# Moving the FFT pieces of an interleaved FFT + MLP kernel: pair distance in one batch, inverse-pair lag and first-stage start in the others

## The chip, the core and the metric

The kernel runs on one NeuronCore of a Trainium2 chip. The metric is the device time of one execution in microseconds (us), lower is better. The core has a matrix engine (TensorE, PE in the profile; its weight loads are listed as PEld), a vector engine (VectorE, DVE), a scalar engine (ScalarE, ACT), GpSimd (POOL) and a queue for transfers (SyncE, SP). Each of them works through its own instructions in order. PSUM is the memory that PE writes; here it is cut into eight banks of 128 x 512 float32.

## The reference

The input is x (8 batches, 3008 positions, 256 channels). A real FFT runs along the positions, the spectrum is multiplied by a filter, and the inverse FFT follows. The result, 24064 rows of 256, goes through a two-layer MLP with PReLU.

```python
def _attn_ref(x, filt_r, filt_i):
    X = np.fft.rfft(x, axis=1)
    F = (filt_r + 1j * filt_i)[None, :, :]
    Y = X * F
    y = np.fft.irfft(Y, n=x.shape[1], axis=1)
    return y.astype(np.float32)

def _moe_ref(x, w_in, w_out, alpha):          # w_in 256 x 2048, w_out 2048 x 256
    h = x @ w_in
    g = np.maximum(h, 0.0) + alpha * np.minimum(h, 0.0)
    return (g @ w_out).astype(np.float32)
```

## The kernel before

**The FFT of a batch** is factored as 3008 = 47 x 64 and done with matmuls in float16. `Fft` has these pieces, each one bank of PSUM from the pool `psF`, which has two banks:

- first stage, `piece_a`, 16 of a batch (letter a): one matmul of 512 columns from `xs` (L164), evicted by ACT into `asb` (L238);
- forward pair, `piece_b`, 12 of a batch (b): two matmuls of 256 columns (L184), then on DVE `ww` (L188) and `uu` (L189), both reading the bank, and two DMAs on POOL that swap the halves of `ww` into `sw` (L191);
- swap-add, `piece_s`: `uu += sw` on DVE (L196), in batches 2 to 7;
- inverse pair, `piece_c`, 12 of a batch (c): two matmuls of 256 columns on `uu` (L209), evicted by ACT into `v` (L238). Batch 1 has no swap-add and uses four matmuls, on `uu` and on `sw`;
- last stage, `piece_d`, 16 of a batch (d): four matmuls of 94 columns (L231), evicted by ACT into `yT` (L238).

Between first stage and forward pairs the data go through DRAM to be transposed: `save_a` writes `asb`, `turn_a` reads it back into `at`. Between inverse pairs and last stage `turn_c` does the same for `v` and `zt`, in four quarters. All of these are DMAs on the SP queue, which also issues the stores of the result. Loads of `xs` and the `sw` swaps are issued on POOL.

**The MLP** runs over 48 blocks of tokens, 12 for each pair of batches (11 of 512 tokens and one of 384), 16 steps to a block, 768 steps in all. In step j, `up(j)` computes one 128-row slice of the hidden layer (two matmuls, L414), into one half of a double bank `hps`; after odd j, ACT copies both halves to `gtb` (L420) and DVE applies the PReLU (two instructions `m`, L423, and an add, L424). `down(j)` does a sixteenth of the second layer of the block before (four matmuls of 256 columns, L433; three after a block of 384). At the middle and the end of a block of 512 its result is evicted by ACT into `osb` (L438) and stored.

**The order of the work** is written out by hand. `plan` maps a step to a list of pieces that are issued ahead of `up` in this step. So a piece of an odd step is evicted ahead of this step's `gtb` copy on ACT, and one of an even step behind the `gtb` copy of the step before; a step that is a multiple of 8 also has the `osb` eviction of the step before in front of it, save in narrow blocks.

`plan_fft(b, a0, ga, ta, b0, gap, add, lag, d0, quarters, x_at)` places batch b: first-stage piece i at `a0 + ga*i`; `turn_a` at `ta`; forward pair kp at `b0 + gap*kp` (rounded to even distances where `add` is set); the swap-add `add` steps and the inverse pair `lag` steps later; `turn_c` of a quarter one step after its third inverse pair; last-stage piece i from `d0` on; `x_at` are the steps in which the next batch's `xs` are loaded. For batches 3 to 7 everything is placed against p = 96(b-1): pairs at p+5, 9, 15, 19, 25, 29, 35, 39, 45, 49, 55 and 59. While these run, the first stage of batch b+1 runs from p+26 on. Batch 0 is handled ahead of the loop and in its first 47 steps.

Of the kernel before, what the change touches and what calls it, by code (L numbers as in the profile page):

```python
# [64 lines left out]
def kernel(  # L65
# [59 lines left out]
    def load_x(b, c):  # L125
        xs = p_x.tile([2 * N1, 8 * D], FP16, name="xs")
        for h in range(2):
            nc.gpsimd.dma_start(out=xs[h * N1 : h * N1 + N1], in_=xrow(b, h, c))  # L128
        return xs
# [314 lines left out]
    def put(step, fn, *args):  # L444
        plan.setdefault(step, []).append((fn, args))

    def plan_fft(b, a0, ga, ta, b0, gap, add, lag, d0, quarters, x_at):
        f = Fft(b)
        for i in range(16):
            put(int(a0 + ga * i), f.piece_a, i, on_act)  # L450
        for c in range(4):
            put(int(a0 + ga * (4 * c + 3)), f.save_a, c)
            if b + 1 < NB:
                put(x_at[c],
                    lambda b=b, c=c: xc.update({(b + 1, c): load_x(b + 1, c)}))
        for q in range(quarters):
            w = NK1 // quarters
            put(ta, f.turn_a, nc.sync, w * q, w * q + w)
        bs = [b0 + (2 * int(gap * kp / 2) if add else int(gap * kp)) for kp in range(12)]
        for kp in range(12):  # L460
            put(bs[kp], f.piece_b, kp)
            if add:
                put(bs[kp] + add, f.piece_s, kp)
            put(bs[kp] + lag, f.piece_c, kp, on_act)
        for q in range(4):
            put(bs[3 * q + 2] + lag + 1, f.turn_c, q)
        for i in range(16):
            put(d0 + min(i, 4) + 2 * max(i - 4, 0), f.piece_d, i, on_act)
# [9 lines left out]
    for i in range(4):  # L478
        put(17 + 3 * i, neg, 6 * i, 6 * i + 6)
    put(29, lambda: nc.gpsimd.dma_start(out=filt_s[64:128], in_=filt_s[0:64]))  # L480
    plan_fft(1, 16, 1, 32, 44, 2.5, 0, 6, 92, 4, (20, 24, 73, 74))
    plan_fft(2, 66, 2, 97, 109, 4.5, 8, 13, 187, 4, (110, 114, 118, 122))
    for b in range(3, NB):
        p = 96 * (b - 1)
        plan_fft(b, p - 70, 2.5, p - 27, p + 5, 5, 8, 13, p + 91, 1, (p + 6, p + 10, p + 16, p + 20))

    prev = None
    step = 0
# [43 lines left out]
```

## Time and profile before

| | |
|---|---|
| median of 3 runs | 799.88 us (799.49 to 799.96) |
| the profiled execution | 799.77 us |
| its span in the profile | 798.0 us |
| granted PE clock, mean | 0.996 |
| start and batch 0, 0 to 38.5 us: PE busy | 31.5 of 38.5 us |
| batch 1's pairs, steps 0 to 79, 38.5 to 126.5 us: PE busy | 83.8 of 88.0 us |
| batch 2's pairs, 126.5 to 220.5 us: PE busy | 92.3 of 94.0 us |
| batches 3 to 6, 220.5 to 602 us: PE busy | 380.1 of 381.5 us |
| batch 7 and the tail, 602 to 798 us: PE busy | 190.4 of 196.0 us |

The shares are those of PE matmuls. A matmul's end is modelled, and matmuls overlap, so short waits show smaller than they are: the distance between the starts of two neighbouring matmuls tells the wait. A line of the page's groups has: line, engine, operation, output and inputs, shapes, count; after the first bar the busy time in us and the mean of one in ns; after the second bar the engine's idle time ahead of these instructions, and what ended most of it. A line of the list of waits has: who waited, for whom, us in total, times, longest. A line of the timeline has: start and length in us, engine, line, operation, tiles, count, and in brackets the idle time before it and its releaser. SP's lines there are instructions that issue transfers; their length is that of issuing, not of the transfer.

### The profile page before, as it was taken

The numbers are of one execution on the slowest core, as the hardware profiler recorded it, in microseconds if no ns is written. First come the engines' busy times: TensorE is split into PE (matmuls) and PEld (weight loads), VectorE is DVE, ScalarE is ACT, GpSimd is POOL, SyncE is SP. The second block draws the span as 40 slices with busy tenths as digits, with TensorE's granted clock in tenths as the row PEclk, the third lists the DMA queues.
The fourth block names the chain that finished last, engine by engine and source line by source line (L and its number), as shares of the span: only waits on it lengthen the run. The fifth ranks groups of instructions, "written<-read, shape, count | busy, mean of one in ns | idle before, by whom it ended". The sixth has DMA issues, their size and how long they took to land.

```text
span 798.0 us, 16169 instructions
## 1 busy us (share of the span) xinstructions
PE 778.0 (97%) x5980; PEld 542.0 (68%) x5980; DVE 646.1 (81%) x1449; ACT 597.9 (75%) x836; POOL 140.6 (18%) x269
## 2 busy tenths in 40 slices
PE   6999999999999999999999999999999999999997
PEld 6756667666667666766667666766667766776665
DVE  4897986799879887798877988799877999777773
ACT  3788668877777887788878877788877867686663
POOL 7510240132103210032102321032100221000000
PEclk9999999999999999999999999999999999999999
DMA  9967358674655447475483545654484243511111
GB/s 191 202 141 193 96 131 209 168 159 129 157 141 116 115 121 177 126 139 132 117 208 81 123 127 139 180 110 114 122 180 116 54 106 85 137 39 28 41 40 53
DMA packets 94247, 100.59 MB, mean 126 GB/s; under 512 B 11320, under 2 KB 81992, under 8 KB 94040
## 3 DMA queue, kind: packets, MB, share of 16 engines
q1 hardware_dynamic: 79512, 68.80, 32.6%
q0 software_dynamic: 14656, 30.75, 19.8%
q8 instruction: 47, 0.77, 0.4%
q14 instruction: 32, 0.26, 0.1%
HBM read 56.26 MB, written 46.66 MB: 129 GB/s over the span
## 4 chain that ended last, share of the span: by engine, by line
PE 87%; ACT 4%; DVE 3%; DMA 3%; issue 2%; SPq 1%; POOL 1%; ACTq 0%; DVEq 0%; POOLq 0%
PE op L433 38%; PE hps L414 37%; PE psF L164 3%; PE psF L231 3%; PE psF L184 2%; PE psF L209 2%; ACT gtb L420 2%; DMA xs<-in_x_dram 1%; DMA a_dram<-asb 1%; DVE ww L188 1%; ACT osb L438 1%; DVE m L423 1%; PE hps L281 1%; DVE uu L189 1%; ACT asb L238 1%
## 5 line engine op out<-in xcount | busy, mean ns | idle before, releaser
L420 ACT ACTIVATE gtb<-hps 128x1024 f16<-128x1024 f32 (+1 forms) x384 | 385.5, 1005 | 127.4 <-PE hps L414 127.0
L433 PE MATMUL op<-wout_s,gtb 128*128 128x256 f16 x3008 | 451.1, 272 | 0.6 <-DVE gtb L424 0.6
L414 PE MATMUL hps<-yT,win_s 128*128 128x512 f16 (+1 forms) x1536 | 449.1, 374 | 0.4 <-ACT gtb L420 0.2
L433 PEld LDWEIGHTS <-gtb 128*128 128x128 f16 x3008 | 293.3, 98 | 189.6 <-DVE gtb L424 0.9
L423 DVE TENSOR_SCALAR m<-gtb,alm_s 128x512 f16<-128x512 f16 (+1 forms) x768 | 237.6, 351 | 100.0 <-ACT gtb L420 98.0
L424 DVE TENSOR_TENSOR gtb<-gtb,m 128x1024 f16<-128x1024 f16 (+1 forms) x384 | 261.6, 681 | 24.8 <-PE hps L414 0.9
L191 POOL DMA_DIRECT2D sw<-ww x168 | 88.0, 529 | 494.4 <-DVE ww L188 485.4
L414 PEld LDWEIGHTS <-win_s 128*128 128x128 f16 x1536 | 145.0, 98 | 31.9 <-issue 4.0
L238 ACT ACTIVATE asb<-psF 96x512 f16<-96x512 f32 x112 | 66.4, 593 | 17.5 <-PE psF L164 17.4
L238 ACT ACTIVATE yT<-psF 128x376 f16<-128x376 f32 x120 | 58.1, 484 | 22.8 <-PE psF L231 22.3
L438 ACT ACTIVATE osb<-op 128x512 f32<-128x512 f32 x96 | 56.1, 584 | 6.1 <-issue 3.2
L188 DVE TENSOR_TENSOR ww<-psF,filts_s 128x512 f16<-128x512 f32 x84 | 57.5, 684 | 0.4 <-PE psF L184 0.3
L189 DVE TENSOR_TENSOR uu<-psF,filt_s 128x512 f16<-128x512 f32 x84 | 57.2, 681 | 0.0
L238 ACT ACTIVATE v<-psF 128x512 f16<-128x512 f32 x84 | 49.9, 594 | 3.3 <-PE psF L209 3.3
L164 PE MATMUL psF<-xs,wf_s 94*96 94x512 f16 x112 | 42.7, 381 | 3.0 <-DVE uu L189 1.3
L231 PE MATMUL psF<-wi_s,zt 96*128 96x94 f16 x504 | 41.9, 204 | 0.9 <-ACT yT L238 0.7
L128 POOL DMA_DIRECT2D xs<-in_x_dram x64 | 34.6, 549 | 26.8 <-PE psF L164 15.0
L231 PEld LDWEIGHTS <-zt 96*128 96x128 f16 x512 | 35.5, 97 | 5.1 <-issue 1.5
L184 PE MATMUL psF<-at,twf_s 128*128 128x256 f16 x168 | 32.0, 272 | 3.0 <-ACT v L238 2.1
L209 PE MATMUL psF<-uu,twi_s 128*128 128x256 f16 x168 | 33.4, 273 | 0.0
L196 DVE TENSOR_TENSOR uu<-uu,sw 128x512 f16<-128x512 f16 x72 | 30.1, 418 | 0.0
L209 PEld LDWEIGHTS <-twi_s 128*128 128x128 f16 x192 | 18.6, 98 | 2.5 <-DVE uu L189 0.4
(57 smaller groups left out, 195.0 us busy)
## 6 DMA issues: line engine op xcount, KB each, us to landing
out_dram<-osb SPq DMA_DIRECT2D x128, 128.0 KB
xs<-in_x_dram POOLq DMA_DIRECT2D x64, 188.0 KB, 4.5
a_dram<-asb SPq DMA_DIRECT2D x28, 384.0 KB
sw<-ww POOLq DMA_DIRECT2D x168, 64.0 KB, 2.1
v_dram<-v SPq DMA_DIRECT2D x112, 96.0 KB
zt<-v_dram SPq DMA_DIRECT2D x28, 384.0 KB
at<-a_dram SPq DMA_DIRECT2D x20, 384.0 KB
at<-a_dram SPq DMA_DIRECT2D x32, 96.0 KB
```

Source lines behind the costliest of these rows:

```text
L164: nc.tensor.matmul(ps[0:96], wf1_s, xs[:, o : o + 512], start=True, stop=True)
L188: nc.vector.tensor_mul(ww, px, filts_s[:, 2 * kp : 2 * kp + 2])
L189: nc.vector.tensor_mul(uu, px, filt_s[:, 2 * kp : 2 * kp + 2])
L191: nc.gpsimd.dma_start(out=sw[o : o + 64], in_=ww[64 - o : 128 - o])
L209: nc.tensor.matmul(pv[:, kh], twi_s[:, k1], u[:, kh], start=u is us[0], stop=u is us[-1])
L231: nc.tensor.matmul(ps[:, m], self.zt[:, 8 * g + 4 * mh + m, dh * 128 : dh * 128 + 128], wi3_s, start=True, stop=True)
L238: nc.scalar.activation(o, i, AF.Copy)
L414: nc.tensor.matmul(self.hps[:, j % 2, 0:tn], win_s[:, kt, j * 128 : (j + 1) * 128], yT[:, kt, self.t0 : self.t0 + tn], start=(kt == 0), st ...
L420: nc.scalar.activation(g[:, :, 0:tn], self.hps[:, :, 0:tn], AF.Copy)
L423: nc.vector.tensor_scalar(m[:, i, 0:tn], g[:, i, 0:tn], 0.0, a, OP.min, OP.mult)
L424: nc.vector.tensor_add(g[:, :, 0:tn], g[:, :, 0:tn], m[:, :, 0:tn])
L433: nc.tensor.matmul(self.op[:, si % 2], self.gts[k][:, 128 * si : 128 * si + 128], wout_s[:, k], start=(k == 0), stop=(k == 15))
```

## The change

Three calls of `plan_fft` get other numbers. No instruction is added or removed on any engine.

```diff
-    plan_fft(1, 16, 1, 32, 44, 2.5, 0, 6, 92, 4, (20, 24, 73, 74))
-    plan_fft(2, 66, 2, 97, 109, 4.5, 8, 13, 187, 4, (110, 114, 118, 122))
+    plan_fft(1, 16, 1, 32, 40, 3, 0, 6, 92, 4, (20, 24, 74, 75))
+    plan_fft(2, 66, 2, 97, 109, 4.5, 8, 12, 187, 4, (110, 114, 118, 122))
     for b in range(3, NB):
         p = 96 * (b - 1)
-        plan_fft(b, p - 70, 2.5, p - 27, p + 5, 5, 8, 13, p + 91, 1, (p + 6, p + 10, p + 16, p + 20))
+        plan_fft(b, p - 68, 2.4, p - 27, p + 5, 5, 8, 12, p + 91, 1, (p + 6, p + 10, p + 16, p + 20))
```

- Batch 1 (the second batch): forward pairs at steps 40, 43, 46, ..., 73 instead of 44, 46, 49, 51, ..., 71; inverse pairs still 6 steps later, so 46 to 79 instead of 50 to 77; `turn_c` at 53, 62, 71, 80 instead of 56, 63, 71, 78. Two loads of `xs` are issued one step later.
- Batches 2 to 7: inverse pairs and `turn_c` one step earlier. The inverse pairs of batches 3 to 7 go from p+18, 22, 28, 32, ... (even steps) to p+17, 21, 27, 31, 37, 41, 47, 51, 57, 61, 67, 71 (odd steps).
- Batches 3 to 7: first-stage pieces, counted by the batch whose pairs run beside them, at p+28, 30, 32, 35, 37, 40, 42, 44, 47, 49, 52, 54, 56, 59, 61, 64 instead of p+26, 28, 31, 33, 36, 38, 41, 43, 46, 48, 51, 53, 56, 58, 61, 63.

## The prediction

> **What bounds the kernel now.** I read the page's busy shares, then who waited for whom on TensorE (PE), then the timeline around those waits, then SyncE's queue.
>
> ```profile
> PE 778.0 (97%) x5980; PEld 542.0 (68%) x5980; DVE 646.1 (81%) x1449; ACT 597.9 (75%) x836; POOL 140.6 (18%) x269
> L423 DVE TENSOR_SCALAR m<-gtb,alm_s 128x512 f16<-128x512 f16 (+1 forms) x768 | 237.6, 351 | 100.0 <-ACT gtb L420 98.0
> L189 DVE TENSOR_TENSOR uu<-psF,filt_s 128x512 f16<-128x512 f32 x84 | 57.2, 681 | 0.0
> ```
>
> PE is the bound; the change leaves its instructions as they are and only reorders them, so time can come only from waits that go or come. A psF bank is freed after a forward pair by `uu`, last of two VectorE (DVE) instructions of 0.68 us, queued behind `m` and the add of the MLP.
>
> ```profile
> PE psF L184 <- ACT v L238: 2.1, 6, 0.3
> PE psF L164 <- DVE uu L189: 1.3, 2, 0.7
> PE psF L184 <- DVE uu L189: 1.0, 1, 1.0
> PE psF L164 <- DMA xs<-in_x_dram: 0.9, 1, 0.9
> ```
>
> Each is a wait for one of the two psF banks (the last too: its instruction names the bank, its releaser ended at 166.17 us, and PE moved at 166.22). These rows count idle time after a modelled matmul end; from start to start a wait costs about 0.16 us more. I use start to start below.
>
> ```profile
> 377.58 1.02 ACT L420 ACTIVATE gtb<-hps 128x1024 f16<-128x1024 f32 x1 [0.45 <-PE hps L414]
> 378.50 0.59 ACT L438 ACTIVATE osb<-op 128x512 f32<-128x512 f32 x1
> 378.98 0.60 ACT L238 ACTIVATE v<-psF 128x512 f16<-128x512 f32 x1
> 379.64 0.38 PE L184 MATMUL psF<-at,twf_s 128*128 128x256 f16 x2 [0.35 <-ACT v L238]
> ```
>
> This is step p+49 of batch 4 (p = 96(b-1) = 288). An inverse pair and a first-stage piece both stood at p+48, right after `gtb` and `osb`; ScalarE (ACT) reached `v` only after both, and the next forward pair waited from 379.12 to 379.64: 0.52 us. It recurs at 189 to 191 us and once in each of batches 3 to 6.
>
> **A step's length on PE.** Up starts at 345.86, down at 346.29, the next piece would be due at 346.73: 0.87 us a step. A first-stage piece, a forward pair and an inverse pair add 0.22 each, a last-stage piece 0.17 (345.69 to 345.86), an inverse pair of batch 1 (four matmuls) 0.43.
>
> **Batches 3 to 7: waits that come.** Forward pairs stay at p+5, 9, 15, 19, ..., 59. Inverse pairs come one step earlier, at p+17, 21, 27, 31, 37, ... In the changed program's order the bank of a pair is asked for again two steps later, not three, at eight places in a batch. The place is visible in the trace already:
>
> ```profile
> 345.45 0.68 DVE L188 TENSOR_TENSOR ww<-psF,filts_s 128x512 f16<-128x512 f32 x1
> 346.05 0.68 DVE L189 TENSOR_TENSOR uu<-psF,filt_s 128x512 f16<-128x512 f32 x1
> 345.86 0.60 PE L414 MATMUL hps<-yT,win_s 128*128 128x512 f16 x2
> 346.79 0.39 PE L209 MATMUL psF<-uu,twi_s 128*128 128x256 f16 x2
> ```
>
> The inverse pair that now starts at 346.79 (p+18) is due at 345.86 in the new order (p+17). Its bank is free at 346.05 + 0.68 = 346.73, plus 0.05 for the semaphore as at 346.79. So it waits 0.9 us, and everything behind it on PE with it. In the old order one more step stood between, so the wait was 0.06.
>
> I did the same for all eight: end of `uu` after the pair's first matmul, read pair by pair from the timeline, plus 0.03 to 0.05, minus PE's way to the next user of the bank. p+17 after the pair at p+15: 2.33 - 2.12, so 0.24 (in batches 4 and 6, whose previous block is the narrow one: 2.89 against 2.01, the 0.9 above). p+21: 2.10 - 2.12, nothing as it stands; but the inverse pair that lay between the up and the pair at p+19 now lies ahead of that up, so PE reaches the pair 0.22 earlier in DVE's cycle: 0.27. p+31: 2.22 - 2.17, and the same shift: 0.27. p+37 (the first-stage piece there): 2.74 - 2.39, less what ACT gains as the piece at p+33 goes: 0.19. p+41: 2.45 - 2.17 and the shift: 0.46. p+47 and p+57: 2.54 - 2.17, but first-stage pieces newly between give PE 0.22 back, and less ACT work ahead of `gtb` some more: 0.10 each. p+61: 2.25 - 2.39, with 0.43 of pieces moved ahead of the up: 0.30. Sum 1.93 us; from the trace unshifted it would be 1.8. In batches 4 and 6 it is 1.93 + 0.66 = 2.59; I keep 0.27 at p+21 there, since the 0.9 us wait just before lets DVE catch up. Batch 7 has no first stage beside it: 0.5. Together 2 x 1.93 + 2 x 2.59 + 0.5 = 9.5.
> Gone: the 0.52 at p+49 in batches 3 to 6, because inverse pairs now stand on odd steps and are evicted ahead of `gtb`: -2.1. Net **+7.4**.
>
> **Batch 2 and the start of batch 3's first stage (+2 steps).** Gone: 1.11 at step 122 (piece and inverse pair in one step, 165.11 to 166.22), 0.52 at 145 and 0.51 at 153 (same pattern as above), 0.28 and 0.07 at 159 and 149: -2.5. New behind `uu`, by the same reckoning: 0.16 at 129 (2.27 after its pair against 2.17), 0.19 at 133 (2.33 against 2.39, with the shift), 0.36 at 151 (2.32 against 2.17, with the shift). At 157 an inverse pair, a forward pair and a piece in one step, where the piece waits for its own step's `v`: that ends 0.11 + 0.27 + 0.04 + 0.59 after the inverse pair starts, PE is there after 0.43: 0.58. Net **-1.2**.
>
> **Batch 1.** Gone: 1.13 at step 46 (a pair two steps after the pair at 44), and 0.80, 0.86, 0.28 at 66, 70, 72: -3.1. With a distance of 3 each bank has three steps. New, by the same rows: 0.24 at 43 (`uu` 3.20 after a pair on an even step, PE's way 2.99); 0.58 at 46, where a last-stage piece, an inverse and a forward pair meet and the forward pair waits for `yT` behind `gtb` (2.05 after the up of step 45 starts, due at 1.47); 0.64 at 70, where a piece waits for its own step's `v` behind `gtb` (2.16 after that up, due at 1.52); 0.28 at 73, behind `gtb`, `osb` and `asb` (2.64, due at 2.36). Net **-1.3**. The first pair's data: SyncE issues the four quarters of `at` from 74.1 to 81.7 us, the first quarter's four from 74.1 to 75.9; the pair moves from 82.3 to 78.5. With 2.1 us to landing (the `sw` row) it is in time by 0.5, with 4.5 (`xs`) late by 1.9. I take 0, as a 96 KB piece is nearest to `sw`'s 64 KB.
>
> **Batch 1's last quarter.** Its writes move from step 78 to 80 in SyncE's queue, past the three stores of the block that ends at step 79; the zt reads queue behind them, and the first last-stage piece (step 92, at 136.76) behind those.
>
> ```profile
> 124.30 1.92 SPq L218 DMA_DIRECT2D v_dram<-v  x4
> 130.16 1.72 SPq L224 DMA_DIRECT2D zt<-v_dram  x4
> 406.42 2.00 SPq L218 DMA_DIRECT2D v_dram<-v  x4
> 410.00 1.73 SPq L224 DMA_DIRECT2D zt<-v_dram  x4
> ```
>
> Stores behind a block's end finish issuing 4.4 us after the start of its last step (104.53 to 108.92), so the writes start at 125.43 + 4.4 = 129.8 instead of 124.3. The reads follow 3.6 to 5.9 later and take 2.1 to 4.5 to land: 135.5 to 140.2 against 136.76, a wait of 0 to 3.4. With the middles, 4.7 and 3.3: **+1.0**.
>
> **Sum.** 7.4 - 1.2 - 1.3 + 1.0 = +5.9 on the profiled run's 799.77 us (span 798.0 and 1.8 around it; 0.1 below the median of 799.88): **805.7 us**. Some 45 new waits, each good to about 0.06 in the same direction, make +-2.5; the zt wait -1.0/+2.4.
>
> The Trainium skill ("TensorE: Matmul & The Clock Gate", section on psum-queue depth-cycling) tells of a kernel whose many short idles between matmul groups let the clock gate swing. The trace here speaks against it: from 80 to 120 us, with four waits of 0.3 to 1.1 us, the granted clock is 1.00.
>
> **Rivals.**
> - *DVE is early enough* (faster). The place is the bank behind `uu`, two steps after a forward pair; it decides at 2.1 us from pair to end of `uu`. If DVE stays under it, the 9.5 and 0.7 (steps 129, 133, 151) and 0.24 fall away: 805.7 - 10.4 = 795.3. For it: two places read 2.10 and 2.22. Against: 2.33 to 2.89 elsewhere. 0.06.
> - *Waits pay for each other*: a wait lets DVE catch up, so that the next one is spared, and half of the 9.5 remains: 801.0. For it: batch 4's 2.89 falls to 2.49 by p+25. Against: ten steps there last 10.4 us and hold 9.3 of DVE work (five times `m` and add at 1.25, two pairs at 1.20, two swap-adds at 0.33), so there is little room. 0.13.
> - *The early transfers are late*: zt at its upper end and the first `at` quarter 1.9 late: 805.7 + 2.4 + 1.9 = 810.0. For it: DMA share is 0.98 to 1.07 at 132 to 139 us. Against: the middles. 0.12.
> - *The clock drops* in the 56-step stretches of batches 3 to 7 to the 0.83 shown at 10 to 20 us: five times 60 us at 0.83 last 61 us longer, 867. 0.01.
> - *The change does less than it says*: the new `a` positions change nothing if banks, not steps, set the order; then only batch 1 and 2 count, 799.77 - 2.5 + 1.0 = 798.3. 0.02.
>
> **Numbers.** Forecast 0.66, from 802.5 to 808.5. Range 802.0 to 809.6: it takes in the size errors and most of the late-transfer case. No change can be told within 0.2%, 798.3 to 801.5. Faster 0.07; same 0.07, about half of the second rival; slower 0.86.
>
> **What would show it.** Waits of PE at L209 and L164 for `uu`, some 0.1 to 0.9 us, at p+17, 21, 31, 37, 41, 61 in each batch, and none of L184 for `v` at p+49; batch 4's and 6's p+17 the longest. Steps 16 to 64 of a batch some 1.4 us longer (2.1 in 4 and 6), the rest of the batch the same; steps 64 to 80 shorter; PE idle at step 92 for zt. It is wrong if those waits for `uu` are missing, or if blocks without FFT pairs change length.

## The result, and the profile after

The changed kernel takes 808.03 us (median of 4 runs, 807.34 to 809.6), the kernel before 799.68 (4 runs): a ratio of 1.0108, interval 1.0091 to 1.0126. It is slower by 8.4 us; the forecast was 805.7, in a range of 802.0 to 809.6. The profiled execution is the quickest of the four, 807.34 us, with a span of 805.5; its first `up` starts 0.9 us earlier than in the profile of before (37.6 against 38.5). The change moves nothing ahead of step 40, and the loads came at the same time: TensorE starts on the last `xs` of batch 0 at 12.79 us, against 12.75. What differs is the granted clock, in the stretch from 10 to 20 us 1.00 here and 0.83 there. So the differences below are taken from the first `up` on.

The same lines of the page, of the changed kernel, and the line of the inverse pair (L209):

```profile
PE 781.5 (97%) x5980; PEld 538.6 (67%) x5980; DVE 647.0 (80%) x1449; ACT 599.1 (74%) x836; POOL 140.4 (17%) x269
L423 DVE TENSOR_SCALAR m<-gtb,alm_s 128x512 f16<-128x512 f16 (+1 forms) x768 | 237.7, 351 | 108.1 <-ACT gtb L420 107.3
L189 DVE TENSOR_TENSOR uu<-psF,filt_s 128x512 f16<-128x512 f32 x84 | 57.2, 682 | 0.0
L209 PE MATMUL psF<-uu,twi_s 128*128 128x256 f16 x168 | 33.7, 274 | 4.9 <-DVE uu L189 4.5
```

The line of the inverse pair in the kernel before:

```profile
L209 PE MATMUL psF<-uu,twi_s 128*128 128x256 f16 x168 | 33.4, 273 | 0.0
```

Counts and durations have not moved; the busy shares tell nothing. What is new is idle time ahead of the inverse pair, which had none before. The list of PE's waits, of the changed kernel:

```profile
PE psF L209 <- DVE uu L189: 4.5, 15, 0.8
PE psF L231 <- DMA zt<-v_dram: 1.6, 1, 1.6
PE psF L164 <- ACT v L238: 1.0, 2, 0.5
PE psF L209 <- DMA sw<-ww: 0.8, 1, 0.8
```

The waits of the forward pairs (L184) for `v` and `uu` are gone, and the inverse pair's waits for `uu` of an earlier pair have come, with one for zt and one for `sw`. The row shows 15 waits, but from start to start there are more: 0.16 us of each wait hide under a matmul's modelled end, and the row holds no idle time under 0.15 us. From start to start, 37 waits from step 120 on end 0.05 to 0.06 us behind the end of a `uu`.

The place that the prediction used, batch 4's p+17 (TensorE's and VectorE's timeline, changed kernel):

```profile
346.18 0.69 DVE L188 TENSOR_TENSOR ww<-psF,filts_s 128x512 f16<-128x512 f32 x1
346.78 0.68 DVE L189 TENSOR_TENSOR uu<-psF,filt_s 128x512 f16<-128x512 f32 x1
...
346.42 0.33 PE L231 MATMUL psF<-wi_s,zt 96*128 96x94 f16 x4
347.52 0.39 PE L209 MATMUL psF<-uu,twi_s 128*128 128x256 f16 x2 [0.77 <-DVE uu L189]
```

`uu` ends at 347.46, the inverse pair starts 0.06 later. The four last-stage matmuls ahead of it take 0.17, so it was due at 346.59: a wait of 0.93 us, forecast 0.9. And p+49 of the same batch, on ScalarE and TensorE:

```profile
380.10 0.60 ACT L238 ACTIVATE v<-psF 128x512 f16<-128x512 f32 x1 [0.50 <-PE psF L209]
380.59 0.58 ACT L238 ACTIVATE asb<-psF 96x512 f16<-96x512 f32 x1
381.07 1.02 ACT L420 ACTIVATE gtb<-hps 128x1024 f16<-128x1024 f32 x1
...
382.04 0.38 PE L184 MATMUL psF<-at,twf_s 128*128 128x256 f16 x2
```

`v` and `asb` are now evicted ahead of `gtb`, two steps before the forward pair, which has no wait left in its line. SyncE's queue around batch 1's last quarter:

```profile
125.74 2.33 SPq L396 DMA_DIRECT2D out_dram<-osb  x3
128.12 2.35 SPq L218 DMA_DIRECT2D v_dram<-v  x4
132.19 2.63 SPq L224 DMA_DIRECT2D zt<-v_dram  x4
```

The three stores stand ahead of the writes. The last stage, due at 134.84, started at 136.64.

Where the time went, as the difference (changed minus before) of the distance between the starts of `up` at both ends of a stretch:

| steps | forecast | measured |
|---|---|---|
| 32 to 80, batch 1's pairs | -1.3 | -1.0 |
| 80 to 96, wait for zt | +1.0 | +1.8 |
| 96 to 176, batch 2's pairs | -1.2 | -0.8 |
| 208 to 256 and 400 to 448, batches 3 and 5 | +1.4 each | +1.6 each |
| 304 to 352 and 496 to 544, batches 4 and 6 | +2.07 each | +2.3 each |
| 592 to 608, batch 7 | +0.5 | +0.5 |
| all other stretches | 0 | 0.0 |
| sum (the rows are rounded) | +5.9 | +8.4 |

### The profile page after: what moved, and what is told of

The parts are those of the page before. It is cut to its first block, busy times and chain, and to the rows that moved or that the text cites. A ratio compares the mean times of both kernels' runs of the same rounds, so it can differ in the third digit from the quotient of the medians.

```text
span 805.5 us, 16163 instructions
## 1 busy us (share of the span) xinstructions
PE 781.5 (97%) x5980; PEld 538.6 (67%) x5980; DVE 647.0 (80%) x1449; ACT 599.1 (74%) x836; POOL 140.4 (17%) x269
## 4 chain that ended last, share of the span: by engine, by line
PE 74%; DVE 12%; ACT 7%; issue 3%; DMA 3%; SPq 1%; POOL 0%; ACTq 0%; DVEq 0%; POOLq 0%
PE op L433 32%; PE hps L414 31%; ACT gtb L420 4%; DVE m L423 4%; DVE gtb L424 3%; PE psF L209 3%; PE psF L164 2%; DVE ww L188 2%; DVE uu L189 2%; PE psF L231 2%; PE psF L184 1%; ACT asb L238 1%; DMA xs<-in_x_dram 1%; DMA v_dram<-v 1%; ACT osb L438 1%
## 5 line engine op out<-in xcount | busy, mean ns | idle before, releaser
L209 PE MATMUL psF<-uu,twi_s 128*128 128x256 f16 x168 | 33.7, 274 | 4.9 <-DVE uu L189 4.5
L184 PE MATMUL psF<-at,twf_s 128*128 128x256 f16 x168 | 32.1, 272 | 0.2
L209 PEld LDWEIGHTS <-twi_s 128*128 128x128 f16 x192 | 16.7, 98 | 12.8 <-DVE uu L189 10.2
```

The lines of the kernel that those rows point to most:

```text
L209: nc.tensor.matmul(pv[:, kh], twi_s[:, k1], u[:, kh], start=u is us[0], stop=u is us[-1])
```

## The experiments

Three theories stood against each other. One: the loss is the psF bank, asked for two steps after a forward pair while `uu` still reads it. Two: it is the inverse pair's own data, the swap-add being a step too late. Three: it is the new places of batch 1's pairs and of the first stage.

**e1: the lag alone undone.**

```diff
-    plan_fft(2, 66, 2, 97, 109, 4.5, 8, 12, 187, ...)
+    plan_fft(2, 66, 2, 97, 109, 4.5, 8, 13, 187, ...)
-        plan_fft(b, p - 68, 2.4, p - 27, p + 5, 5, 8, 12, p + 91, ...)
+        plan_fft(b, p - 68, 2.4, p - 27, p + 5, 5, 8, 13, p + 91, ...)
```

> The changed kernel with one part undone: inverse pairs of batches 2 to 7 again 13 steps behind the forward ones. Theory 1 (the loss is the psF bank, asked for two steps after a forward pair while uu still reads it) and theory 2 (the loss is the inverse pair's own data, the swap-add being too late by a step) both expect the PE waits for uu at p+17 to p+61 to vanish and 799.5 to 801.5 us. Theory 3 (the new places of batch 1's pairs and of the first stage cost the time) expects 806 or more.

Measured: 800.82 us, ratio to before 1.0018 (1.0008 to 1.0027). In its list no inverse pair waits for `uu`, and a wait of 0.55 us at p+49 is back in each of batches 2 to 6, now of the first-stage piece there for `v`. So 7 of the 8.4 us hang on the one step of lag, and theory three falls.

**e2: the lag alone done,** on the kernel before (13 to 12 in the same two calls).

> The kernel before with this part alone: lag 12 in batches 2 to 7, all else as before. Theories 1 and 2: 807 to 810 us, with the waits for uu two steps behind the forward pairs, at least as many as in the changed kernel. Theory 3: 799 to 801.

Measured: 809.05 us, 1.0123 (1.0107 to 1.0138). That is no less than with the whole change: the two intervals overlap, but the profiles tell them apart, as batches 3 and 5 lose 2.07 us each, 4 and 6 lose 2.8, against 1.6 and 2.3 with the first stage moved too. The new first-stage places soften the loss; they do not cause it.

**e3: batch 1's part alone.** The first line of the change, on the kernel before.

> The kernel before with batch 1's part alone (pairs from step 40 in distances of 3, two xs loads a step later). From the two traces: about 1.0 us gained between steps 32 and 80, 1.8 us lost at step 92 where the last stage waits for zt; so 800.5 us, +0.8. If the zt wait belongs to the whole change and not to batch 1, 798.7.

Measured: 801.49 us, 1.0020 (1.0007 to 1.0033), an interval that takes in the +0.8 us expected. In its profile steps 32 to 80 gain 1.33 us, the zt wait costs 2.3 and steps 96 to 176 lose 0.2, in sum +1.2. The zt wait was 1.8 to 2.3 us in the profiles of the five kernels that have it.

**e4: the first stage's part alone,** `p - 68, 2.4` on the kernel before.

> The kernel before with the first stage's part alone (from step 28 of the period in distances of 2.4), lag 13. Theories 1 and 2: the 1.1 us at step 122 goes, single waits of 0.3 to 0.5 us where a piece and an inverse pair share a step stay or move; 798.5 to 801. Theory 3: 804 or more.

Measured: 799.45 us, 0.9994 (0.9984 to 1.0004): no change that can be told. The wait at step 122 has gone, and one of 1.1 us at step 140 has come, where a piece waits for `v`.

**e5: two steps more lag, same parity.** It tells the bank from a rival on ScalarE: on odd steps `v` is evicted ahead of `gtb` and so delays the MLP's chain.

```diff
-    plan_fft(2, 66, 2, 97, 109, 4.5, 8, 12, 187, ...)
+    plan_fft(2, 66, 2, 97, 109, 4.5, 8, 14, 187, ...)
-        plan_fft(b, p - 68, 2.4, p - 27, p + 5, 5, 8, 12, p + 91, ...)
+        plan_fft(b, p - 68, 2.4, p - 27, p + 5, 5, 8, 14, p + 91, ...)
```

> The changed kernel with lag 14: the inverse pairs still on odd steps, so their evictions still stand ahead of the gtb copy on ScalarE, but two steps later, with four steps from a forward pair to the next user of its bank. Theory 1: the eight waits for uu of a batch go; new ones of 0.6 us where an inverse pair, a forward pair and a first-stage piece share a step (p+49, p+59; as step 157 of the changed kernel); 801 to 804 us. A rival (it is the eviction ahead of gtb on odd steps that delays the MLP's chain): waits as in the changed kernel, 807 or more.

Measured: 805.68 us, 1.0078 (1.0062 to 1.0093), between the two expectations. The list decides. TensorE's waits from 230 to 330 us; from start to start, too, no other of 0.1 us or more is there:

```profile
PE psF L164 <- ACT v L238: 0.9, 2, 0.5
PE psF L184 <- ACT yT L238: 0.4, 1, 0.4
```

Not one is for `uu`, and from step 120 on none of 0.1 us or more ends right behind a `uu`, though the evictions stand ahead of `gtb` as in the changed kernel; the rival falls. What is left are three places in a batch where three pieces meet in one step: 0.5 us at p+19 (last stage, inverse and forward pair), which I had not counted, and 0.63 at p+49 and p+59. The 0.5 us at p+19 in five batches make 2.6 us; the time lies 1.7 us above the expected range.

**e6: one transfer moved.**

```diff
-            put(bs[3 * q + 2] + lag + 1, f.turn_c, q)
+            put(bs[3 * q + 2] + lag + (0 if b == 1 and q == 3 else 1), f.turn_c, q)
```

> The changed kernel with one step of one transfer moved: batch 1's last turn_c in step 79, with its last inverse pair, instead of step 80, so that its four writes stand ahead of the three stores in SyncE's queue. If the wait for zt at step 92 is the queue's order: the writes start about 3.4 us earlier, the wait of 1.8 us goes, 806.2 us. If it is DMA bandwidth: the wait stays above 1 us, 807 to 808.

Measured: 806.12 us, 1.0085 (1.0068 to 1.0102). SyncE's queue in this kernel:

```profile
124.48 2.18 SPq L218 DMA_DIRECT2D v_dram<-v  x4
128.70 1.73 SPq L224 DMA_DIRECT2D zt<-v_dram  x4
130.47 2.36 SPq L396 DMA_DIRECT2D out_dram<-osb  x3
```

The writes now go ahead of the stores, and TensorE waits for nothing from 120 to 150 us. The zt wait was the queue's order, not bandwidth.

**e7: the swap-adds two steps earlier,** `add` 6 for 8 in the changed kernel. Theories one and two expect opposite signs.

> The changed kernel with the swap-adds of batches 2 to 7 six steps behind the forward pairs instead of eight, all matmuls where they were. Theory 2 (the inverse pair waits for its own swap-add): with the sum two steps earlier the waits at p+17 to p+61 go, 799 to 802 us. Theory 1 (it waits for the bank that uu of the pair two steps before still reads): the swap-add now stands right ahead of ww and uu of the pairs at p+15, 25, 35, 45 and 55, so the waits grow by up to 0.33 us there; 810 to 815.

Measured: 814.14 us, 1.0182 (1.0167 to 1.0197). TensorE's waits for psF from 250 to 345 us, and VectorE's timeline at p+15 of batch 3, with the swap-add right ahead of `ww`:

```profile
PE psF L209 <- DVE uu L189: 1.2, 4, 0.4
PE psF L164 <- DVE uu L189: 0.7, 2, 0.3
```

```profile
253.34 0.42 DVE L196 TENSOR_TENSOR uu<-uu,sw 128x512 f16<-128x512 f16 x1
253.68 0.68 DVE L188 TENSOR_TENSOR ww<-psF,filts_s 128x512 f16<-128x512 f32 x1
254.28 0.68 DVE L189 TENSOR_TENSOR uu<-psF,filt_s 128x512 f16<-128x512 f32 x1
```

The waits at p+17, 37, 47 and 57 grow from 0.28, 0.19, 0.20 and 0.17 us to 0.61, 0.53, 0.53 and 0.50: by 0.33 to 0.34 each, which is the 0.34 from the swap-add's start to that of `ww`. Those at p+21, 31 and 61, with no swap-add newly in front, stay; that at p+41 falls by 0.08. Theory two falls: the inverse pair's own data came earlier, and it waited longer. The bank it is. The count of waits of 0.1 us or more, from start to start and from step 120 on, that end 0.05 to 0.06 us behind the end of a `uu` says the same. It is 37 in the changed kernel and in e7, 32 in e2, 2 in e1 (0.14 us each), none in e5 and in the kernel before.

**e8 and e9: a schedule from what was found.** Lag 13, so three steps from a forward pair to the next user of its bank; first-stage pieces from p-71 in distances of 2.55, of which none shares p+48 with an inverse pair; in e8 also batch 1's pairs from step 41 in distances of 2.5, inverse pairs 8 steps behind.

```diff
-    plan_fft(1, 16, 1, 32, 44, 2.5, 0, 6, 92, 4, (20, 24, 73, 74))
+    plan_fft(1, 16, 1, 32, 41, 2.5, 0, 8, 92, 4, (20, 24, 74, 75))
...
-        plan_fft(b, p - 70, 2.5, p - 27, p + 5, 5, 8, 13, p + 91, ...)
+        plan_fft(b, p - 71, 2.55, p - 27, p + 5, 5, 8, 13, p + 91, ...)
```

> A new schedule by the rule that the runs support: lag 13 (three steps from a forward pair to the next user of its bank), first stage from p-71 in distances of 2.55, so that no piece shares step p+48 with an inverse pair, and batch 1's pairs from step 41 in distances of 2.5 with inverse pairs 8 steps behind. Theory 1: the 0.53 us at p+49 of batches 2 to 6, the 1.1 us at 122 and most of the waits at 46 to 72 go, none for uu of the pair two steps before comes, and the last writes of batch 1 stay at or ahead of step 78: 793.5 to 796 us. If waits on PE move elsewhere instead: 799 or more.

> The kernel before with the first stage's new places alone (from p-71 in distances of 2.55). Theory 1: 2.1 us from p+49 in batches 3 to 6 and 1 to 2 us in batch 2; 795 to 797.5 us. If waits on PE move elsewhere: 799 or more.

Measured: e8 793.77 us, 0.9920 (0.9904 to 0.9937); e9, without batch 1's line, 795.67 us, 0.9943 (0.9928 to 0.9958). Both beat both kernels. In e8's list no piece of the FFT waits for `uu`, zt or `sw`. From start to start small ones are left behind `uu`: 0.26 us at step 43, two steps after the pair at 41, and 0.20 at 49. The one row that is not in the list of before is this:

```profile
PE psF L164 <- ACT v L238: 0.7, 2, 0.5
```

Its larger part is at step 66, 0.68 us start to start, where a first-stage piece of batch 2 meets two pieces of batch 1.

## Why the prediction was right

The direction, the mechanism and the range held. The change cost 2.4 us more than forecast, 0.9 of it in batches 3 to 7, 0.8 at zt, 0.4 in batch 2 and 0.3 in batch 1; all four erred in the same direction, so the time came out near the upper end of the forecast. Step by step:

- *Waits behind `uu` two steps after a pair, in batches 3 to 7* (+9.5): right in place and in kind, by e1, e2, e5 and e7. Each of the eight is there, and ends 0.05 to 0.06 us behind the end of the `uu` in question. At p+17, 21, 31, 37, 41, 47, 57 and 61 they were, by the length of their steps, 0.28, 0.33, 0.35, 0.19, 0.51, 0.20, 0.17 and 0.25 us against 0.24, 0.27, 0.27, 0.19, 0.46, 0.10, 0.10 and 0.30; 0.95 at p+17 in batches 4 and 6 against 0.9. The step's size was some 0.35 us short in a batch; in the table 0.2 of it shows, since small waits of before went too, 0.07 us at p+19 among them. A part of it is the time from the end of `uu` to TensorE's start, which the sums leave out in places: at p+31, 2.22 - 2.17 + 0.22 is 0.27 without it, and at p+47 and p+57 `uu` ended 2.27 us after the pair instead of 2.54, just what the prediction gave back, against a way of 2.17, so 0.10 without it. At p+41, 2.45 - 2.17 + 0.22 makes 0.50, not 0.46.
- *The wait at p+49 goes* (-2.1): right; no wait is left there.
- *Batch 2* (-1.2): 0.8 measured. The new waits at 129, 133, 151 and 157 were right within 0.1 us. A wait of 0.2 at step 112 was not on the list, and its cause stays open: `uu` of the pair at 109 ends 2.7 us after the pair in both kernels, and the last-stage piece of step 112 starts at 154.94 in the changed one, 0.14 behind that end (154.80). In the kernel before it started at 154.87, ahead of that end (154.91), so there it had the other bank.
- *Batch 1* (-1.3): 1.0 measured. The waits at 43, 70 and 73 were right within 0.03 us. At step 46 the forward pair was to lose 0.58 us to `yT`; TensorE lost 0.94, and most of it one instruction earlier: the first inverse pair's second matmul waited for `sw` (1.03 us from 84.02 to 85.05, 0.92 more than the usual 0.11). POOL issued its two swaps from 80.49 to 81.54, as SyncE finished issuing the sixteen reads into `at` (80.58), and they landed 4.0 us after their issue instead of the 2.1 of their row; that the reads held them up is not shown. The prediction did not ask whether `sw` would be there. The five other profiles with these places of batch 1's pairs lost 0.61 to 0.65 there, near the forecast, though in them too an inverse matmul waited for `sw` first (0.2 to 0.5 us in their lists).
- *The first pair's data*: no wait at step 40, as taken.
- *zt* (+1.0): 1.8, inside its bounds of 0 to 3.4; e6 shows that it is the stores ahead in the queue. The writes started at 128.12 and the reads 4.1 us later, but 4.4 us passed from the reads' issue to the last stage's start (132.19 to 136.64), near the bound of 4.5 and not the middle of 3.3.

Of the rivals, "DVE is early enough" and "the change does less than it says" fall with the waits at all eight places, and "waits pay for each other" too: after 0.95 us at p+17 the next wait was 0.33 us, as after 0.28. The pieces of data that came late (zt, `sw`) were the third rival's kind, "the early transfers are late", and worth 0.8 + 0.4 us over the forecast. The clock did not drop: the granted mean is 0.999, with 38 waits of 0.15 to 0.93 us between steps 120 and 600, 4.6 us or more apart. The swing of the clock that the Trainium skill ("TensorE: Matmul & The Clock Gate", section on psum-queue depth-cycling) tells of did not show at waits this short and this far apart.

## What to carry to other kernels

Where a piece that is spread over another loop takes one of two buffers, the lag that counts is not from a piece to the consumer of its data, but from a piece to whichever comes next for its buffer; read the end of the last reader from the timeline and lay it against the new distance before moving anything by a step. Which piece comes next for a buffer has to be read from the built program: the two banks are not always taken in turn, as step 112 shows. When the consumer sits on the bound engine, waits of 0.2 to 0.5 us at eight places in a batch make most of a loss of 1% of the time, and no busy share shows it. A transfer moved by two steps is moved past everything that its queue gets in these steps, here three stores, and pays for all of them.

## What the runs showed of the hardware that was not expected

A small swap on POOL's queue (64 KB) comes late now and then: TensorE waited for `sw` at step 46 in the changed kernel (0.8 us in its row), but also at step 60 in the profiles of e4 (0.3) and e9 (0.4), whose batch 1 is that of before, where no such wait showed. The page's median of 2.1 us to landing is no bound: the longest of the 168 swaps took 4.7 us in the changed kernel and 4.1 in the one before. And a VectorE instruction that reads a full bank has a length of 0.68 us in the trace, but the next one starts 0.60 after it (346.18 to 346.78): summing lengths would overstate each round of the queue by some 0.08 us an instruction.
